# A new opening sequence for a block-sparse attention and mixer kernel, and two normalising steps that both read PSUM

## The chip, the cores and the metric

The kernel runs on one core of a Trainium2 chip. The metric is the device time of one execution in microseconds: 315.58 as the median of 13 runs before the change (314.32 to 317.63).

TensorE (PE in the profile) multiplies matrices into PSUM, VectorE (DVE) and ScalarE (ACT) read PSUM and write SBUF, GpSimd (POOL) works on SBUF alone, and SyncE (SP) issues most of the DMA transfers. Each engine executes its instructions in the order of its own queue.

## The reference

Two stages follow each other. Attention first, for 4 batches, 8 heads, 768 positions and head size 64, with positions in 24 blocks of 32:

```
scores = q k^T / 8
mask   = neighbouring blocks, first and last block (as row or column), 3 sampled blocks per row block
attn   = softmax(where(mask, scores, -1e9))
x      = attn v                      # heads side by side: [4, 768, 512]
```

Then a mixer:

```
u   = x + transpose(transpose(x) U V)       # U 768x32, V 32x768
out = u + relu(u w1) w2                      # w1 512x2048, w2 2048x512
```

## The kernel before

**Attention.** The work goes by pairs of heads: 16 pairs, 4 to a batch. The head size of 64 is filled up to 128 rows: 24 rows beside the data hold one-hot rows on the q side and mask rows on the k side, so that the product of the two gives score plus mask bias. For each head there are six "slots" g, each 128 keys: `scores` (L308) multiplies them with all 768 queries, ScalarE takes the exponential into `est`, and `Pair.av` (L344) multiplies `est` with v into the PSUM tile `pav`, of which there is one buffer. Column 64 of v is all ones, so that the sum of the exponentials comes with the product. After the sixth group, VectorE takes the reciprocal (L360), writes the normalised values `xf` in fp32 from PSUM (L362), and casts them to the fp16 tile `xh` (L366). The next head's first `av` matmul waits until `pav` has been read.

**Mixer.** `mix` (L368) multiplies U with `xh`. `ut` (L377) builds the transposed `u` for one pair, in two halves: three matmuls of `xh` against the identity matrix `id16` (a transpose that adds up in fp32), then V times the result of `mix`, all into one PSUM tile, which VectorE casts to `uT` (L390). The MLP of a batch is a list of steps: 32 of `w1` (four matmuls each, relu by ScalarE and VectorE in turn, L409 and L411) and 24 of `w2`; every fourth of the latter ends in an output sum on VectorE (L428) and a store on SP (L429).

**Order.** TensorE's instructions stand in program order (a manual schedule); on the other engines a scheduler orders them, by the order of the program and its own estimate of when each is ready. One loop walks over 192 slots. In each it traces `scores`, then what `plan` holds for the slot, then at most one entry of `mixer` (`mix` at 4 slots after the pair's end, `ut` at 6 and 7), then as many MLP steps of the batch before as are due. `AVSLOT` gives the slot, counted from the head's first, in which each of the six `av` groups stands: 3, 4, 5, 6, 7, 7. In batch 0 there are no MLP steps.

**Loads.** q, k and v come as fp32 and GpSimd casts them to fp16 (L144, L154). Pairs 0 to 5 are transposed by TensorE (`front_pe`, L296, into `qres` and `kres`, two sets), pairs 6 to 15 by DMA transposes that SP issues (`front`, L286). The load buffers are two deep, and a load waits on SP until its buffer is free. GpSimd issues the loads of the weights.

**Opening.** ScalarE's queue issues the sampled blocks and the small constants (mask, block numbers, and the one-hot rows twice); SP issues the identity and pair 0's q and k, one head at a time. Ten matmuls on zeros (L482 to L484) run first on TensorE. VectorE zeroes the first set of `qres` and `kres`, GpSimd the second; VectorE copies the one-hot rows (L189), then runs the mask chain (L194 three times, L199). `first_front` (L204) casts, transposes and copies q or k of one head of pair 0; `mask_rows` (L221) multiplies the mask into the rows of `kres`; `second_set` (L236) copies mask and one-hot rows to the second set.

Of the kernel before, what the change touches and what calls it, by code (L numbers as in the profile page):

```python
# [16 lines left out]
P = 128  # L17
# [3 lines left out]
def kernel(  # L21
# [44 lines left out]
    oh_np = np.zeros((P, T, D), dtype=np.float16)  # L66
    oh_np[cols % P, cols // P, blk] = 1.0

    small_np = np.zeros((D + NB, 2 * NB + 2 + S), dtype=np.float16)
    small_np[:NB] = np.concatenate(  # L70
        [ms_np.view(np.float16), ii[:, None].astype(np.float32).view(np.float16), ohT_np],
        axis=1,
    )
    small_np[D:, 2 * NB + 2 :] = ohT_np
    eye_np = np.eye(P, dtype=np.float16)

    small_dr = nc.inline_tensor(small_np, name="small_const")
# [25 lines left out]
    def psm(shape, dtype):  # L103
        return psmp.tile(shape, dtype, tag="pm", name="pm")
# [3 lines left out]
    small = consts.tile([P, 2 * NB + 2 + S], FP16)  # L108
    ms = small[0:NB, 0 : 2 * NB].bitcast(FP32)
    iota = small[0:NB, 2 * NB : 2 * NB + 2].bitcast(FP32)  # L110
    ohr = small[:, 2 * NB + 2 :]
    ohT = ohr[0:NB]
    sb = consts.tile([P, NB, 3, 2], I32)
    vts = [consts.tile([P, H, T, DV], FP16, name=f"vt{i}") for i in range(2)]
    qst = [consts.tile([P, 2, T, P], FP16, name=f"qst{i}") for i in range(NST)]
# [46 lines left out]
            [NB, NB * 6]  # L162
        ),
    )
    nc.scalar.dma_start(out=small[0 : D + NB, :], in_=small_dr.ap())
    nc.sync.dma_start(out=id16, in_=eye_dr.ap())
    lds = {}
    for h in range(2):
# [6 lines left out]
            )  # L175

    warm = consts.tile([P, 512], FP16)
    nc.vector.memset(warm, 0.0)
    bias = consts.tile([P, 2, D], FP16)
    nc.vector.memset(bias, 0.0)  # L180
    for i, eng in ((0, nc.vector), (1, nc.gpsimd)):
        for res in (qres, kres):
            eng.memset(res[i], 0.0)
    for vt in vts:
        nc.gpsimd.memset(vt[:, :, :, D : D + 1], 1.0)
    nc.gpsimd.memset(Ut, 0.0)
    nc.gpsimd.memset(Vt, 0.0)
    for h in range(2):
        nc.vector.tensor_copy(out=qres[0][mrows[h], h, :], in_=ohr[mrows[h], :])  # L189

    a01 = consts.tile([P, NB], FP32)
    prev = ms
    for r in range(3):
        nc.vector.scalar_tensor_tensor(  # L194
            out=a01[0:NB], in0=sb[0:NB, :, r, 0], scalar=iota,
            in1=prev, op0=ALU.is_equal, op1=ALU.max,
        )
        prev = a01[0:NB]
    nc.vector.tensor_scalar(  # L199
        out=bias[0:NB, :, 0:NB], in0=a01[0:NB, None].broadcast_to([NB, 2, NB]),  # L200
        scalar1=-MASK_BIAS, scalar2=MASK_BIAS, op0=ALU.mult, op1=ALU.add,
    )

    def first_front(h, n):  # L204
        nm, res = (("qld", qres), ("kld", kres))[n]
        copy = nc.scalar.copy if (h, n) == (0, 1) else nc.vector.tensor_copy
        dst = sts[0, nm][:, :, h]
        if h == 0:
            copy(out=dst, in_=lds[nm][:, h])
        else:  # L210
            nc.gpsimd.tensor_copy(out=dst, in_=lds[nm][:, h])
        pt = psm([P, S], FP16)
        for t in range(T):
            nc.tensor.transpose(  # L214
                out=pt[0 : (h + 1) * D, t * P : (t + 1) * P],
                in_=sts[0, nm][:, t, 0 : h + 1].rearrange("p h d -> p (h d)"),
                identity=id16,
            )
        copy(out=res[0][drows[h], h, :], in_=pt[drows[h], :])  # L219

    def mask_rows():  # L221
        pks = [psvp.tile([P, HS], FP32, tag="pv", name="pv"), psm([P, HS], FP32)]
        for c in range(2):
            nc.tensor.matmul(
                pks[c],
                bias[0:NB].rearrange("k a z -> k (a z)"),
                ohT[:, c * HS : (c + 1) * HS],
                start=True, stop=True,
            )
        for h in range(2):  # L230
            for c in range(2):
                nc.vector.tensor_copy(
                    out=kres[0][mrows[h], h, c * HS : (c + 1) * HS], in_=pks[c][mrows[h]]
                )

    def second_set():  # L236
        for h in range(2):
            nc.gpsimd.tensor_copy(out=qres[1][mrows[h], h, :], in_=ohr[mrows[h], :])
            nc.vector.tensor_copy(out=kres[1][mrows[h], h, :], in_=kres[0][mrows[h], h, :])

    def mask_columns():
        def both(ap):
# [93 lines left out]
    class Pair:  # L336
        def __init__(self, i, bt):
            self.b, self.hp = divmod(i, HP)
            self.bt = bt
            self.ests = {}  # L340
            self.xh = xpool.tile([P, T, P], FP16, tag="xh", name="xh", bufs=3)
            self.ch = slice(self.hp * P, (self.hp + 1) * P)

        def av(self, h, g):  # L344

            head = 2 * self.hp + h
            if g == 0:
                self.pav = psvp.tile([P, T, D + 1], FP32, tag="pv", name="pv")
            pav, est = self.pav, self.ests.pop((h, g))
            for sc in range(T):  # L350
                nc.tensor.matmul(  # L351
                    pav[:, sc, :],
                    est[:, sc * P : (sc + 1) * P],
                    vts[self.b % 2][:, head, g, 0 : D + 1],
                    start=(g == 0 and sc == 0), stop=(g == T - 1),
                    skip_group_check=True,
                )
            if g == T - 1:
                rcp = misc.tile([P, T], FP32, tag="rcp", name="rcp")
                nc.vector.reciprocal(out=rcp, in_=pav[:, :, D])  # L360
                xs = self.bt.xf[:, :, head * D : (head + 1) * D]
                nc.vector.tensor_tensor(  # L362
                    out=xs, in0=pav[:, :, 0:D],
                    in1=rcp[:, :, None].broadcast_to([P, T, D]), op=ALU.mult,
                )
                nc.vector.tensor_copy(out=self.xh[:, :, h * D : (h + 1) * D], in_=xs)  # L366

        def mix(self):  # L368
            pa = psm([P, P], FP32)
# [6 lines left out]

        def ut(self, c):  # L377
            pu = psm([P, HS], FP32)
            for j in range(3):
                nc.tensor.matmul(  # L380
                    pu[:, j * P : (j + 1) * P], self.xh[:, 3 * c + j, :], id16,
                    start=(j == 0), stop=False, skip_group_check=True,
                )
            nc.tensor.matmul(  # L384
                pu,
                self.bt.a16[:, self.ch],
                Vt[:, 3 * c : 3 * c + 3, :].rearrange("r t p -> r (t p)"),
                start=False, stop=True, skip_group_check=True,
            )
            nc.vector.tensor_copy(  # L390
                out=self.bt.uT[self.hp][:, c * HS : (c + 1) * HS], in_=pu
            )


    def mlp_steps(b, bt):
# [54 lines left out]

    LAG = 8
    SLOTS = HP * 2 * T
    AVSLOT = (3, 4, 5, 6, 7, 7)
    queue = []
    plan = {}
    mixer = []
# [22 lines left out]
            since_open += 1  # L479

    with tc.manual_schedule(engines={mybir.EngineType.PE}):
        for _ in range(10):  # L482
            pw = psm([P, 512], FP32)
            nc.tensor.matmul(pw, warm[:, 0:P], warm, start=True, stop=True)  # L484
        first_front(0, 0)
        mask_rows()
        first_front(0, 1)
        at(0, lambda: first_front(1, 0))
        at(1, lambda: first_front(1, 1))
        load_v(0)  # L490
        load_qk(1)
        load_v(1)
# [86 lines left out]
```

The softmax here doesn't subtract the row's maximum and nothing guards it: scores larger than these inputs give would overflow.

## Time and profile before

| what | value |
|---|---|
| median of 13 runs | 315.58 us |
| the profiled execution | 315.29 us, span 313.5 us |
| busy share of the span: TensorE, ScalarE, VectorE, GpSimd | 96%, 57%, 42%, 17% |
| first score on TensorE, first exponential on ScalarE | 12.02 us, 12.88 us |
| bytes moved by DMA | 38.15 MB, 122 GB/s on average |

The page cuts the span into 40 equal slices, one digit each: the busy share in tenths. A group line names the source line, the engine, the operation, the tiles written and read, the shapes and the count; then the busy time in us, the mean duration of one in ns, and the idle time of the engine just before such instructions, with what ended it. A timeline line gives start and duration in us, then the same names; an idle time and its cause stand in brackets. PEld is the loading of weights into TensorE, which lies beside its matmuls. The chain that ended last is followed backwards from the last instruction, at each step to what released it.

### The profile page before, as it was taken

What the parts mean: (1) busy time and instruction counts of PE and PEld (TensorE: products, weight loads), DVE (VectorE), ACT (ScalarE), POOL (GpSimd) and SP (SyncE); (2) the same over time, 40 slices, a digit from 0 to 9 for tenths busy, and PEclk for the clock granted to TensorE, in tenths of its full rate; (3) what the DMA queues carried; (4) which work ended last, traced back from release to release, by engine and by line L of the source; (5) the groups of instructions that cost most, each with busy time, mean ns of one, the idle gap of its engine ahead of it and who ended that gap; (6) DMA issues with size and microseconds to landing.
All of it is one profiled execution on the core that took longest, in us unless ns stands there. A gap on an engine that the chain in (4) does not pass through costs nothing.

```text
span 313.5 us, 6739 instructions
## 1 busy us (share of the span) xinstructions
PE 302.0 (96%) x2782; PEld 185.1 (59%) x2782; DVE 132.3 (42%) x273; ACT 180.0 (57%) x259; POOL 54.5 (17%) x73
## 2 busy tenths in 40 slices
PE   5799999999999999999999999999999999999994
PEld 1467766666665655666665655666665555565442
DVE  5757656544433323444442233445342233443111
ACT  2399999567856555677765555686765550332000
POOL 9692754013320203020201102000000000000000
PEclk9599999999999999999999999999999999999999
DMA  7999999999943747080625125070500101000111
GB/s 217 350 313 239 318 170 134 125 206 258 341 153 81 190 94 211 33 185 18 136 70 102 69 70 132 33 102 2 100 2 33 37 33 69 33 3 0 67 69 67
DMA packets 51238, 38.15 MB, mean 122 GB/s; under 512 B 32887, under 2 KB 47591, under 8 KB 51207
## 3 DMA queue, kind: packets, MB, share of 16 engines
q1 hardware_dynamic: 48384, 33.37, 42.5%
q0 software_dynamic: 2688, 4.19, 8.3%
q8 instruction: 22, 0.36, 0.5%
q10 hardware_dynamic: 135, 0.16, 0.2%
q14 instruction: 9, 0.07, 0.1%
HBM read 27.75 MB, written 6.29 MB: 109 GB/s over the span
## 4 chain that ended last, share of the span: by engine, by line
PE 87%; ACT 7%; DVE 2%; DMA 1%; issue 1%; ACTq 0%; DVEq 0%
PE pm L420 26%; PE pm L401 26%; PE psc L313 17%; PE pv L351 9%; ACT est L319 7%; PE pm L371 2%; PE pm L380 2%; PE pm L384 2%; PE pm L418 2%; DMA small<-small_const 1%; DVE a L194 1%; DVE of L428 1%; PE pm L214 1%; DVE qres L189 0%; DVE xf L362 0%
## 5 line engine op out<-in xcount | busy, mean ns | idle before, releaser
L319 ACT ACTIVATE est<-psc 128x768 f16<-128x768 f32 x192 | 151.3, 810 | 65.0 <-PE psc L313 64.7
L420 PE MATMUL pm<-w2t,tT 128*128 128x512 f16 x384 | 95.1, 379 | 0.0
L401 PE MATMUL pm<-uT,w1t 128*128 128x384 f16 x512 | 94.5, 326 | 0.0
L351 PEld LDWEIGHTS <-est 128*128 128x128 f16 x1152 | 55.6, 97 | 21.3 <-DVE xf L362 1.9
L401 PEld LDWEIGHTS <-w1t 128*128 128x128 f16 x512 | 47.0, 98 | 26.7
L351 PE MATMUL pv<-vt,est 128*128 128x65 f16 x1152 | 60.9, 193 | 0.1
L313 PE MATMUL psc<-aq,ak 128*128 128x384 f16 x240 | 58.5, 326 | 0.0
L411 DVE TENSOR_SCALAR tT<-pm 128x384 f16<-128x384 f32 x64 | 35.7, 557 | 47.6 <-PE pm L401 37.9
L420 PEld LDWEIGHTS <-tT 128*128 128x128 f16 x384 | 35.2, 98 | 33.0
L409 ACT ACTIVATE tT<-pm 128x384 f16<-128x384 f32 x64 | 31.3, 489 | 33.1 <-PE pm L401 17.6
L313 PE MATMUL psc<-qres,kres 128*128 128x384 f16 x144 | 35.8, 333 | 2.7 <-ACT kres L219 0.9
L428 DVE TENSOR_TENSOR of<-xf,pm 128x512 f32<-128x512 f32 x24 | 16.5, 687 | 50.7 <-PE pm L420 50.7
L313 PEld LDWEIGHTS <-ak 128*128 128x128 f16 x240 | 23.4, 98 | 21.9
L390 DVE CAST uT<-pm 128x384 f16<-128x384 f32 x32 | 17.7, 553 | 27.5 <-PE pm L384 27.3
L144 POOL CAST qst<-qld 128x768 f16<-128x768 f32 x10 | 8.3, 828 | 97.0 <-DMA aq<-qst 59.3
L360 DVE RECIPROCAL rcp<-pv 128x6 f32<-128x6 f32 x32 | 6.3, 196 | 32.8 <-PE pv L351 32.0
L313 PEld LDWEIGHTS <-kres 128*128 128x128 f16 x144 | 13.7, 99 | 8.7 <-issue 3.5
L362 DVE TENSOR_TENSOR xf<-pv,rcp 128x384 f32<-128x384 f32 x32 | 17.8, 557 | 1.1
L154 POOL CAST vt<-vld 128x768 f16<-128x768 f32 x16 | 13.5, 843 | 23.5 <-PE pv L351 10.4
L366 DVE CAST xh<-xf 128x384 f16<-128x384 f32 x32 | 15.2, 475 | 0.4
L380 PE MATMUL pm<-id,xh 128*128 128x128 f16 x96 | 10.6, 219 | 0.0
L384 PE MATMUL pm<-Vt,a 128*128 128x384 f16 x32 | 10.4, 326 | 0.0
(63 smaller groups left out, 121.4 us busy)
## 6 DMA issues: line engine op xcount, KB each, us to landing
vld<-in_v_dram SPq DMA_DIRECT2D x16, 384.0 KB, 5.3
out_dram<-of SPq DMA_DIRECT2D x24, 256.0 KB, 2.0
qld<-in_q_dram SPq DMA_DIRECT2D x15, 384.0 KB, 4.7
kld<-in_k_dram SPq DMA_DIRECT2D x15, 384.0 KB, 5.5
w1t<-in_moe_w_ch_dram POOLq DMA_DIRECT2D x4, 512.0 KB, 8.3
w2t<-in_moe_w_ch_dram POOLq DMA_DIRECT2D x4, 512.0 KB, 15.2
qld<-in_q_dram SPq DMA_DIRECT2D x2, 192.0 KB, 3.7
kld<-in_k_dram SPq DMA_DIRECT2D x2, 192.0 KB, 3.7
```

Source lines behind the costliest of these rows:

```text
L313: nc.tensor.matmul(psc[:, c, 0:HS], kT[:, h, g * P : (g + 1) * P], qT[:, h, c * HS : (c + 1) * HS], start=True, stop=True,)
L319: nc.scalar.activation(out=est.rearrange("k (c n) -> k c n", c=2), in_=psc[:, :, 0:HS], func=AF.Exp, scale=0.125,)
L351: nc.tensor.matmul(pav[:, sc, :], est[:, sc * P : (sc + 1) * P], vts[self.b % 2][:, head, g, 0 : D + 1], start=(g == 0 and sc == 0), stop= ...
L362: nc.vector.tensor_tensor(out=xs, in0=pav[:, :, 0:D], in1=rcp[:, :, None].broadcast_to([P, T, D]), op=ALU.mult,)
L380: nc.tensor.matmul(pu[:, j * P : (j + 1) * P], self.xh[:, 3 * c + j, :], id16, start=(j == 0), stop=False, skip_group_check=True,)
L384: nc.tensor.matmul(pu, self.bt.a16[:, self.ch], Vt[:, 3 * c : 3 * c + 3, :].rearrange("r t p -> r (t p)"), start=False, stop=True, skip_gr ...
L390: nc.vector.tensor_copy(out=self.bt.uT[self.hp][:, c * HS : (c + 1) * HS], in_=pu)
L401: nc.tensor.matmul(pt, w1t[:, cc, jj * P : (jj + 1) * P], bt.uT[cc][:, c * HS : (c + 1) * HS], start=(cc == 0), stop=(cc == NCC - 1),)
L409: nc.scalar.activation(out=dst, in_=pt, func=AF.Relu)
L411: nc.vector.tensor_scalar_max(out=dst, in0=pt, scalar1=0.0)
L420: nc.tensor.matmul(hold[sc], bt.tT[jj][:, sc * P : (sc + 1) * P], w2t[:, jj, :], start=False, stop=(jj == NJJ - 1),)
L428: nc.vector.tensor_add(out=of, in0=bt.xf[:, sc, :], in1=hold[sc])
```

## The change

The opening is written anew. The small constants hold the one-hot rows once and are issued by SP ahead of everything else. The order of the opening is written by hand for TensorE, VectorE and ScalarE. VectorE zeroes all four tiles of `qres` and `kres`. The cast of q's first head stands ahead of the mask chain. ScalarE copies the one-hot rows of head 0, and one of the four pieces of the mask rows. Matmuls on zeros stand at three places: 8 first, 1 behind the q transposes, 3 behind the k transposes. The second set's one-hot and mask rows are copied by four DMAs on SP.

In `av`, both normalised results are now made from PSUM, the fp16 one first. For pairs 8 to 14 a tile `xT` is filled from `xh` by a DMA transpose on SP; `ut` then leaves the three identity matmuls out, and VectorE adds `xT` as it reads PSUM. `AVSLOT` is 3, 4, 5, 6, 6, 7.

```diff
-    small_np = np.zeros((D + NB, 2 * NB + 2 + S), dtype=np.float16)
-    small_np[:NB] = np.concatenate(
+    small_np = np.concatenate(
...
-    small_np[D:, 2 * NB + 2 :] = ohT_np
...
-    nc.scalar.dma_start(out=small[0 : D + NB, :], in_=small_dr.ap())
+    nc.sync.dma_start(out=small[0:NB, :], in_=small_dr.ap())
     nc.sync.dma_start(out=id16, in_=eye_dr.ap())
...
-    for i, eng in ((0, nc.vector), (1, nc.gpsimd)):
-        for res in (qres, kres):
-            eng.memset(res[i], 0.0)
...
+    def first_cast(h, n, copy):
+        nm = ("qld", "kld")[n]
+        copy(out=sts[0, nm][:, :, h], in_=lds[nm][:, h])
+
+    def first_turn(h, n):
         pt = psm([P, S], FP16)
         for t in range(T):
             nc.tensor.transpose(
...
+    def first_rows(h, n, pt, copy):
+        copy(out=(qres, kres)[n][0][drows[h], h, :], in_=pt[drows[h], :])
+
+    with tc.manual_schedule(
+        engines={mybir.EngineType.PE, mybir.EngineType.DVE, mybir.EngineType.Activation}
+    ):
+        nc.vector.memset(warm, 0.0)
+        nc.vector.memset(bias, 0.0)
+        for res in (*qres, *kres):
+            nc.vector.memset(res, 0.0)
+        pw = pscp.tile([P, 2, 512], FP32, tag="psc", name="psc")
+
+        def keep_warm(n):
+            for _ in range(n):
+                nc.tensor.matmul(pw[:, 0], warm[:, 0:P], warm, start=True, stop=True)
+
+        keep_warm(8)
+        nc.scalar.copy(out=qres[0][mrows[0], 0, :], in_=ohT)
+        first_cast(0, 0, nc.vector.tensor_copy)
+        ptq = first_turn(0, 0)
+        keep_warm(1)
+        prev = ms
+        for r in range(3):
+            nc.vector.scalar_tensor_tensor(
...
+        nc.vector.tensor_scalar(
...
+        first_rows(0, 0, ptq, nc.vector.tensor_copy)
+        first_cast(0, 1, nc.scalar.copy)
         pks = [psvp.tile([P, HS], FP32, tag="pv", name="pv"), psm([P, HS], FP32)]
         for c in range(2):
             nc.tensor.matmul(
...
+        first_rows(0, 1, first_turn(0, 1), nc.scalar.copy)
+        keep_warm(3)
         for h in range(2):
             for c in range(2):
-                nc.vector.tensor_copy(
+                (nc.scalar.copy if (h, c) == (0, 1) else nc.vector.tensor_copy)(
                     out=kres[0][mrows[h], h, c * HS : (c + 1) * HS], in_=pks[c][mrows[h]]
                 )
+        nc.vector.tensor_copy(out=qres[0][mrows[1], 1, :], in_=ohT)
+
+    def first_front(n):
+        first_cast(1, n, nc.gpsimd.tensor_copy)
+        first_rows(1, n, first_turn(1, n), nc.vector.tensor_copy)
 
     def second_set():
         for h in range(2):
-            nc.gpsimd.tensor_copy(out=qres[1][mrows[h], h, :], in_=ohr[mrows[h], :])
-            nc.vector.tensor_copy(out=kres[1][mrows[h], h, :], in_=kres[0][mrows[h], h, :])
+            nc.sync.dma_start(
+                out=qres[1][mrows[h], h, :], in_=small_dr.ap()[:, 2 * NB + 2 :]
+            )
+            nc.sync.dma_start(out=kres[1][mrows[h], h, :], in_=kres[0][mrows[h], h, :])
...
+            self.xT = None
+            if 2 * HP <= i < NPAIR - 1:
+                self.xT = xpool.tile([P, T, P], FP16, tag="xT", name="xT")
...
-                xs = self.bt.xf[:, :, head * D : (head + 1) * D]
-                nc.vector.tensor_tensor(
-                    out=xs, in0=pav[:, :, 0:D],
-                    in1=rcp[:, :, None].broadcast_to([P, T, D]), op=ALU.mult,
-                )
-                nc.vector.tensor_copy(out=self.xh[:, :, h * D : (h + 1) * D], in_=xs)
+                for dst in (
+                    self.xh[:, :, h * D : (h + 1) * D],
+                    self.bt.xf[:, :, head * D : (head + 1) * D],
+                ):
+                    nc.vector.tensor_tensor(
+                        out=dst, in0=pav[:, :, 0:D],
+                        in1=rcp[:, :, None].broadcast_to([P, T, D]), op=ALU.mult,
+                    )
+                if h == 1 and self.xT is not None:
+                    nc.sync.dma_start_transpose(
+                        self.xT, self.xh.rearrange("p t c -> p (t c)")
+                    )
...
-            for j in range(3):
+            for j in range(3 if self.xT is None else 0):
...
-                start=False, stop=True, skip_group_check=True,
-            )
-            nc.vector.tensor_copy(
-                out=self.bt.uT[self.hp][:, c * HS : (c + 1) * HS], in_=pu
-            )
+                start=(self.xT is not None), stop=True, skip_group_check=True,
+            )
+            dst = self.bt.uT[self.hp][:, c * HS : (c + 1) * HS]
+            if self.xT is None:
+                nc.vector.tensor_copy(out=dst, in_=pu)
+            else:
+                nc.vector.tensor_tensor(
+                    out=dst, in0=pu,
+                    in1=self.xT[:, 3 * c : 3 * c + 3, :].rearrange("c t p -> c (t p)"),
+                    op=ALU.add,
+                )
...
-    AVSLOT = (3, 4, 5, 6, 7, 7)
+    AVSLOT = (3, 4, 5, 6, 6, 7)
...
-        for _ in range(10):
-            pw = psm([P, 512], FP32)
-            nc.tensor.matmul(pw, warm[:, 0:P], warm, start=True, stop=True)
-        first_front(0, 0)
-        mask_rows()
-        first_front(0, 1)
-        at(0, lambda: first_front(1, 0))
-        at(1, lambda: first_front(1, 1))
+        at(0, lambda: first_front(0))
+        at(1, lambda: first_front(1))
```

## The prediction

> **What bounds the kernel now.** I read the page's slices first, then the chain that ended last, then a table by stretches, then timelines of the places that the change touches. Slices and chain:
>
> ```profile
> PE   5799999999999999999999999999999999999994
> ACT  2399999567856555677765555686765550332000
> PEclk9599999999999999999999999999999999999999
> PE 87%; ACT 7%; DVE 2%; DMA 1%; issue 1%; ACTq 0%; DVEq 0%
> ```
>
> A slice is 7.84 us. TensorE is full from the third slice to the end; in slices 3 to 7 ScalarE is full beside it; only the first two slices have room. The stretches agree (columns: time, busy PE, PEld, DVE, ACT, POOL, granted clock, DMA share, GB/s):
>
> ```profile
> 8.00:16.00 8.00, 5.92 (x40) 3.64 (x40) 6.07 (x12) 2.98 (x4) 5.29 (x8) 0.57 1.06 350
> 24.00:55.00 31.00, 29.91 (x421) 21.74 (x418) 20.09 (x45) 29.75 (x42) 15.06 (x19) 1.00 1.09 215
> 55.00:265.00 210.00, 209.85 (x1977) 129.60 (x1975) 82.26 (x176) 129.62 (x187) 19.87 (x24) 1.00 0.48 108
> ```
>
> So there are three regimes. Until the first exponential nothing is full: it is a chain of latencies, partly at a clock of 0.57. From there to 55 us ScalarE sets the pace (one exponential per about 0.72 us), with TensorE taking over at pair boundaries. After 55 us TensorE never stops. A microsecond gained at the start is kept to the end if no load is late; one TensorE microsecond removed after 55 us is one off the end.
>
> The start, ScalarE's and VectorE's timelines (start, duration, operation, wait):
>
> ```profile
> 6.32 1.24 DVE L194 SCALAR_TENSOR_TENSOR a<-sb,small 24x24 f32<-24x24 int32 x1
> 7.48 0.34 DVE L209 CAST stqld<-qld 128x384 f16<-128x384 f32 x1
> 7.75 1.52 DVE L194 SCALAR_TENSOR_TENSOR a<-sb,small,a 24x24 f32<-24x24 int32 x2
> 9.31 0.18 DVE L199 TENSOR_SCALAR bias<-a 24x48 f16<-24x48 f32 x1
> ...
> 11.17 0.79 ACT L219 COPY kres<-pm 64x768 f16<-64x768 f16 x1 [5.32 <-PE pm L214]
> 12.88 0.81 ACT L319 ACTIVATE est<-psc 128x768 f16<-128x768 f32 x1 [0.91 <-PE psc L313]
> 14.16 0.81 ACT L319 ACTIVATE est<-psc 128x768 f16<-128x768 f32 x1 [0.47 <-PE psc L313]
> 15.44 0.81 ACT L319 ACTIVATE est<-psc 128x768 f16<-128x768 f32 x1 [0.47 <-PE psc L313]
> ```
>
> The reader is to see the order: wait for the small constants (VectorE idle 2.32 us), two one-hot copies, mask chain to 9.49, mask matmuls from 9.54, k transposes, k rows on ScalarE, scores at 12.02, exponential at 12.88. The q load had landed at 4.83, k's first head at 5.31. The next two exponentials come 1.28 us apart because TensorE runs at half clock until 15.3.
>
> **What the Trainium skill says.** "TensorE: Matmul & The Clock Gate", Part 1: the clock doubles only after a window of about 3.4 us of activity and halves after an idle one. The trace agrees: full at 5.1 to 8.5 us, half until 15.3, in steps of 3.41. "SBUF — State Buffer", SBUF: two separate sides: GpSimd and a VectorE instruction with two SBUF inputs share a port pair under an exclusive lock. The trace agrees: the same 24x24 instruction of L194 takes 0.24 us alone and 1.24 beside a GpSimd copy. "VectorE: DVE Perf Modes", Why PSUM operands drop a tier: an fp32 PSUM operand leaves one element a cycle, so an fp16 output is not cheaper than an fp32 one; L362 shows 0.557 us.
>
> **The change, part by part.**
>
> *Start.* Small constants become 39 KB instead of 141 and go first on SP, so every load behind them issues one slot later (1.15−0.74 = 0.41 us) but has 0.10 MB less ahead (0.3 us at 340 GB/s): q lands at about 4.95, k at 5.4. VectorE takes all four zeroings (4×0.70, over by about 4.1, before q), then the q cast (0.34): 5.3. The one-hot copies leave VectorE and GpSimd; ScalarE's copy (by "ScalarE: Activation LUTs", What ACT_TABLE_LOAD costs, 0.186 + 768×0.83 ns, an estimate of 0.83 us) lies between the table load's end (2.98) and k's landing: nothing, unless the constants land after 4.6, then its lateness delays the k cast. Mask chain: uncontended 3×0.24 + 0.18 + gaps = 1.0, with GpSimd's casts of head 1 (0.50 and 0.71, landing about 5.9 and 6.4) in its way 2.2; I take 1.3, bias at 6.6 against 9.49. Two mask matmuls 0.6, k transposes 0.52 (full clock) to 0.85, take 0.7: 7.9. ScalarE's k rows 0.79: 8.75; the three warming matmuls lie under them. Scores 0.5 to 0.8: first exponential at about 9.5, against 12.88, **−3.4 us**. ScalarE's extra row copy (a 384-wide cast takes 0.49 in L409) lies under the scores; if the scores wait for it, +0.5. The two slots to the third exponential take 1.45 at full clock, 2.56 now; I take 1.95, **−0.6**. Sum −4.0; ends −2.5 (half clock, locked chain) and −5.3.
>
> Does a load stop it? Data needed earlier by 4.0: pair 1's q cast ends at 10.56 and its transposes start at 16.62 (6.1 us of room); v 8.97 against 15.60; Vt's cast ends at 19.05, first used at 27.0 (8 us). The four new SP copies of `second_set` wait for the mask rows (about 8.6), and SP's queue stands behind them: loads of pair 2 issued at 7.89 now go at about 10.3, costing 2.4 of Vt's 8. GpSimd's queue issues the first weight load behind pair 2's k cast, so it slips as much; the weights landed at 33.5 and are first used at 56.5. All fit, with 1.6 us left at worst (Vt). GpSimd loses 2×1.38 of zeroing and 1.8 of copies, before any use.
>
> *Batch 0, normalising.* The fp16 copy now comes from PSUM (0.557) ahead of the fp32 one (0.557) instead of a cast after it, so the PSUM tile of weighted values comes free 0.59 us later. What waits is the next head's first matmul on TensorE:
>
> ```profile
> 32.83 0.20 DVE L360 RECIPROCAL rcp<-pv 128x6 f32<-128x6 f32 x1 [1.98 <-PE pv L351]
> 33.06 0.56 DVE L362 TENSOR_TENSOR xf<-pv,rcp 128x384 f32<-128x384 f32 x1
> 33.67 0.26 PEld L351 LDWEIGHTS <-est 128*128 128x128 f16 x6 [0.18 <-DVE xf L362]
> ```
>
> Four of the eight heads of batch 0 have no room (0.06 to 0.09 us), four have 0.43. The new slot list moves the fifth group of products one slot ahead, so the sixth ends about 0.17 earlier where ScalarE sets the pace. Net 0.42 for the tight heads, of which the next score's wait (0.17) absorbs a part: 4×0.25 = **+1.0**; ends 0 and +2.4 (4×0.59, none absorbed).
>
> *From 55 us.* Of the 24 heads there, all but two that hand over to another head with work behind have 0.86 us or more between L362's end and the next use, more than 0.59. The two at 129 and 200 us stall already, as VectorE takes a `uT` cast and an output sum between:
>
> ```profile
> 197.95 0.20 DVE L360 RECIPROCAL rcp<-pv 128x6 f32<-128x6 f32 x1 [0.99 <-PE pv L351]
> 198.28 0.56 DVE L390 CAST uT<-pm 128x384 f16<-128x384 f32 x1
> 199.15 0.69 DVE L428 TENSOR_TENSOR of<-xf,pm 128x512 f32<-128x512 f32 x1 [0.31 <-PE pm L420]
> 199.87 0.56 DVE L362 TENSOR_TENSOR xf<-pv,rcp 128x384 f32<-128x384 f32 x1
> ```
>
> 2×0.59 = **+1.2** if that order stays, 0 if it goes. VectorE's extra 0.2 us per head is covered by its idle time (61% after 55 us).
>
> *`ut` of pairs 8 to 14.* Three identity matmuls leave each of 14 calls:
>
> ```profile
> 142.01 0.33 PE L380 MATMUL pm<-id,xh 128*128 128x128 f16 x3
> 142.18 0.33 PE L384 MATMUL pm<-Vt,a 128*128 128x384 f16 x1
> ```
>
> Start to start it is 0.17 us (the 219 ns of one is mostly latency): 14×0.17 = **−2.35**. In their place stand seven transposes on SP. The nearest rows are the transposes of twice the size: 1.4 to 1.8 us to issue, landing 3.8 to 4.1 after. I take 0.9 to issue and 3.5 to land. From `xh` ready to VectorE's `uT` step are 5.7 to 6.4 us now, so they are hidden by 1.3 to 2 us if SP is free. Behind a load or store already waiting on SP (at 156.3, 175.3, 193.3, 246.6) they land about 0.5 us late; VectorE then holds relus, which three PSUM buffers cover. I take **+0.3**, ends 0 and +3. The sum read with `xT` costs VectorE as much as the cast did (0.56).
>
> Sum: −4.0+1.0+1.2−2.35+0.3 = −3.85 on a span of 313.5. The profiled execution took 315.29, so 311.4; the median of the runs is 0.3 above it: **311.7 us**.
>
> **Rivals.**
> (B) The start gains only half: the chain is locked by GpSimd, the clock stays low, or scores wait for ScalarE's second copy. For it: the locked 1.24 above, a pause of TensorE between q transposes and bias; against: warming matmuls in that gap. −2.0 in place of −4.0, the rest unchanged: **313.7**.
> (C) The PSUM hold costs nothing and the start gains all: −5.3−2.35 = −7.65, **307.9**; against it stand the measured 0.06 to 0.09 us of room.
> (D) Slower: the `xT` transposes sit on SP behind stores, VectorE waits in front of relus, and TensorE runs out of PSUM buffers. For it: SP holds stores for output sums (170.7 to 182.3). Three buffers of 0.65 us of products each, less the one in use, cover 1.3 us of lateness beyond the room. Without the xT term my sum is −4.15, so it decides from a TensorE loss of (4.15+0.95)/7 = 0.73 us a pair, a lateness of 2.0 us beyond the room; at 2.5 the loss is 7×1.2 = 8.4: +4.3, **319.9**. Against it: a transpose far behind the store would wait for a sum queued after the step that waits for it, and loads end before 160 us.
> (E) Nothing measurable: stalls eat the gain: **315.6**.
>
> **How the numbers follow.** A no-change measurement tells about 0.3%, 0.95 us. Main case 0.58 (309.8 to 313.0), B 0.18 (313 to 314.6), C 0.11 (under 309.8), E 0.05, D 0.08. The range 308.6 to 314.5 leaves out D, E and C's lower half. Faster 0.87, same 0.05, slower 0.08.
>
> **What would show it.** First exponential at 9 to 10 us and half clock gone by about 12; bias before 7; all eight heads of batch 0 with a wait of TensorE for the second normalising step of 0.2 to 0.6 us; 2742 TensorE matmuls (2782−42+2 for warming); no VectorE wait for `xT`. Wrong, if the first exponential comes after 11, if a load keeps GpSimd late for pair 1, or if VectorE waits for `xT` by more than 2 us a pair.

## The result and the profile after

The changed kernel takes 307.69 us as the median of 11 runs (307.25 to 309.41), against 315.69 for the kernel before (48 runs, 314.06 to 318.33). The ratio is 0.9743, 95% interval 0.9722 to 0.9764. The forecast was 311.7 with a range of 308.6 to 314.5: the sign is right, but the gain of 8.0 us is twice the forecast 3.9, and the time lies below the range. The profiled execution took 307.92 us with a span of 306.0, so the spans differ by 7.55 us.

The page of the changed kernel, slices (7.65 us each) and the chain that ended last:

```profile
PE   8999999999999999999999999999999999999995
ACT  3999998486855655777766455777765540332000
PEclk9999999999999999999999999999999999999999
PE 89%; ACT 6%; DVE 3%; issue 1%; ACTq 0%
```

The first two slices of TensorE, 5 and 7 tenths before, are 8 and 9 now, and the clock has no low slice (its records begin at 6.53 us). The same three stretches as before, from the changed kernel's table (columns: time, busy PE, PEld, DVE, ACT, POOL, granted clock, DMA share, GB/s):

```profile
8.00:16.00 8.00, 7.49 (x95) 5.32 (x96) 5.47 (x11) 7.84 (x13) 5.62 (x8) 1.00 1.03 327
24.00:55.00 31.00, 29.56 (x394) 20.76 (x393) 19.93 (x44) 28.31 (x40) 15.67 (x21) 1.00 1.06 239
55.00:265.00 210.00, 209.78 (x1935) 128.27 (x1934) 83.27 (x175) 128.31 (x185) 20.01 (x25) 1.00 0.47 115
```

From 8 to 16 us ScalarE is busy for 7.84 us where it had 2.98, at a clock of 1.00 instead of 0.57. After 55 us TensorE is full as before, so whatever is gained there must be matmuls that are gone.

Where the 7.55 us come from is read by laying the two traces side by side slot by slot: the start of the same `scores` matmul on TensorE, after minus before.

| stretch | after minus before, cumulative | in this stretch |
|---|---|---|
| slot 0 (first score) | −3.93 | −3.93 |
| slot 4 | −5.40 | −1.47 |
| slot 57 (batch 0 and the first slots of batch 1) | −5.09 | +0.31 |
| slot 114 | −5.09 | 0.00 |
| slot 191, behind pairs 8 to 14 | −7.37 | −2.28 |
| end of the span | −7.55 | −0.18 |

Of the 5.40, the first exponential accounts for 4.25 (12.88 to 8.63 us) and the two behind it for 1.15. The last 0.18 is outside the change's reach as far as the trace shows: TensorE's last matmul is 7.37 earlier, and the last store, behind the last output sum, took 3.02 us in place of 3.20.

The start in the changed kernel, timelines of VectorE, then ScalarE (start, duration, operation, wait):

```profile
4.35 0.30 DVE L184 CAST stqld<-qld 128x384 f16<-128x384 f32 x1
...
4.83 0.52 DVE L219 SCALAR_TENSOR_TENSOR a<-sb,small,a 24x24 f32<-24x24 int32 x2
5.38 0.17 DVE L224 TENSOR_SCALAR bias<-a 24x48 f16<-24x48 f32 x1
```

```profile
2.54 1.28 ACT L213 ACT_TABLE_LOAD   x1 [2.54 <-DMA small<-small_const]
...
8.63 8.79 ACT L336 ACTIVATE est<-psc 128x768 f16<-128x768 f32 x12
```

q is cast at 4.35, the mask chain runs without any lock (0.52 us for two of its instructions), the bias stands at 5.55 instead of 9.49, and from 8.63 ScalarE runs twelve exponentials without a gap. The three between which 1.28 us lay before are now 0.71 and 0.69 apart.

### The profile page after: what moved, and what is told of

Its sections match the earlier page's. It is cut to its first block, busy times and chain, and to the rows that moved or that the text cites. A ratio compares the mean times of both kernels' runs of the same rounds, so it can differ in the third digit from the quotient of the medians.

```text
span 306.0 us, 6678 instructions
## 1 busy us (share of the span) xinstructions
PE 298.4 (98%) x2742; PEld 181.1 (59%) x2742; DVE 129.8 (42%) x271; ACT 181.6 (59%) x261; POOL 49.7 (16%) x69
## 4 chain that ended last, share of the span: by engine, by line
PE 89%; ACT 6%; DVE 3%; issue 1%; ACTq 0%
PE pm L433 27%; PE pm L452 27%; PE psc L330 17%; PE pv L371 11%; ACT est L336 5%; PE pm L397 2%; PE pm L450 2%; PE pm L410 1%; PE psc L210 1%; DVE xf L385 1%; DVE xh L385 1%; PE pm L406 1%; DVE of L460 1%; PE pm L189 0%; DVE rcp L380 0%
## 5 line engine op out<-in xcount | busy, mean ns | idle before, releaser
L330 PE MATMUL psc<-qres,kres 128*128 128x384 f16 x144 | 35.1, 325 | 2.0 <-ACT est L336 1.0
L385 DVE TENSOR_TENSOR xh<-pv,rcp 128x384 f16<-128x384 f32 x32 | 17.8, 555 | 0.9
L330 PEld LDWEIGHTS <-kres 128*128 128x128 f16 x144 | 12.8, 97 | 7.5 <-issue 3.4
L418 DVE CAST uT<-pm 128x384 f16<-128x384 f32 x18 | 10.0, 553 | 16.8 <-PE pm L410 16.8
L420 DVE TENSOR_TENSOR uT<-pm,xT 128x384 f16<-128x384 f32 x14 | 7.8, 558 | 12.2 <-PE pm L410 12.2
L141 POOL CAST kst<-kld 128x768 f16<-128x768 f32 x10 | 8.3, 827 | 13.3 <-DMA kld<-in_k_dram 9.0
```

The lines of the kernel that those rows point to most:

```text
L141: last = nc.gpsimd.tensor_copy(out=dst, in_=ld)
L330: nc.tensor.matmul(psc[:, c, 0:HS], kT[:, h, g * P : (g + 1) * P], qT[:, h, c * HS : (c + 1) * HS], start=True, stop=True,)
L385: nc.vector.tensor_tensor(out=dst, in0=pav[:, :, 0:D], in1=rcp[:, :, None].broadcast_to([P, T, D]), op=ALU.mult,)
L418: nc.vector.tensor_copy(out=dst, in_=pu)
```

## The experiments

Each edit is made on the changed kernel and shown against it. "Slot n" is again the start of that slot's score. The four runs of one version lie up to 3.1 us apart, so small terms are read from slots of the profiles, one for each version.

**The normalising alone undone.**

```diff
-                for dst in (
-                    self.xh[:, :, h * D : (h + 1) * D],
-                    self.bt.xf[:, :, head * D : (head + 1) * D],
-                ):
-                    nc.vector.tensor_tensor(out=dst, in0=pav[:, :, 0:D], ...)
+                xs = self.bt.xf[:, :, head * D : (head + 1) * D]
+                nc.vector.tensor_tensor(out=xs, in0=pav[:, :, 0:D], ...)
+                nc.vector.tensor_copy(out=self.xh[:, :, h * D : (h + 1) * D], in_=xs)
```

> The changed kernel (307.69 us) with the normalising of before: fp32 result from PSUM first, then a cast of it to fp16. Theory 1 (the longer hold of the PSUM tile really costs only what the slot-by-slot comparison shows in batch 0, 0.3 us, because the scores queued behind the waiting products stand 0.2 to 0.4 us early): 0.2 to 0.4 us faster than the changed kernel, 307.3 to 307.5, and TensorE's wait for the normalising falls from 3.4 to about 1.9 us. Theory 2 (the hold costs 1.0 us as predicted, and the new slot list gives 0.7 us back): 1.0 us faster, 306.7.

Measured: 309.05 us, ratio 0.9776 (0.9721 to 0.9831); span 306.2, 0.25 longer than with the new normalising. From slot 6 to slot 57 the old order loses 0.14 against the new. A further 0.44 is lost between slots 57 and 129 and none of it in batch 0: `xh` is now the second of the two results, its transpose starts later, and VectorE waits in front of `uT`. In the changed kernel, then in this run, VectorE at pair 9:

```profile
155.26 0.56 DVE L420 TENSOR_TENSOR uT<-pm,xT 128x384 f16<-128x384 f32 x1 [0.22 <-PE pm L410]
```

```profile
156.12 0.56 DVE L418 TENSOR_TENSOR uT<-pm,xT 128x384 f16<-128x384 f32 x1 [1.18 <-PE psc L330]
```

The wait is put down to TensorE, but V's matmul started at 154.90 in the first and at 154.81 in the second; what is later is `xT`, whose transpose was issued at 151.24 instead of 150.48 and whose last packets moved until 155.57 instead of 153.54. (The moment at which it counts as landed isn't recorded in this run.) So the new order costs nothing that shows here, since 0.14 is less than such profiles differ by (see below), and it pays once where a transposed copy waits for it. The forecast had a loss.

**The slot list alone undone.**

```diff
-    AVSLOT = (3, 4, 5, 6, 6, 7)
+    AVSLOT = (3, 4, 5, 6, 7, 7)
```

> The changed kernel with the old slot list (3, 4, 5, 6, 7, 7). Theory 1 (the slot list moves nothing, since the last group ends at the same place in TensorE's order): within 0.3 us of 307.69. Theory 2 (the slot list pays for the longer hold): 0.7 us slower, 308.4, the loss within the first 57 slots.

Measured: 308.61 us, ratio 0.9752 (0.9708 to 0.9797); span 306.5. From slot 6 to slot 57 it loses 0.79 us, and nothing after. The waits between 8 and 57 us, in the changed kernel and then in this run (engine, line, what it waited for: us, times, longest):

```profile
PEld L371 <- DVE xf L385: 2.4, 5, 0.5
```

```profile
PEld L371 <- DVE xf L385: 3.3, 5, 0.7
PE pv L371 <- DVE xf L385: 1.4, 5, 0.3
```

With the old list the next head's products wait for the PSUM tile, on the matmuls too. The slot list keeps most of the longer hold of the tile off TensorE; it gives something with the short hold too, as the next run shows.

**The opening alone**: old normalising, old slot list, no `xT`.

```diff
-            if 2 * HP <= i < NPAIR - 1:
+            if False:
...
-    AVSLOT = (3, 4, 5, 6, 6, 7)
+    AVSLOT = (3, 4, 5, 6, 7, 7)
```

(and the edit of the first experiment)

> The new opening alone: normalising, slot list and identity matmuls as before. If the parts add up as the slot-by-slot comparison has them (start -5.4 us, batch 0 +0.3, transposes -2.35): 309.7 to 310.1 us, and in batch 0 the slots 6 to 57 take as long as in the kernel before. If the new slot list and the new normalising belong together (old slot list with new normalising lost 0.8 us in these slots, new slot list with old normalising nothing): the same time, but then batch 0 here must be as fast as in the changed kernel or up to 0.3 us faster, not 0.65 us slower as plain adding of the two single runs would have it.

Measured: 310.84 us, ratio 0.984 (0.9807 to 0.9874); span 308.9, which is 4.6 below the kernel before. At slot 6 it is ahead of the kernel before by 5.17, at slot 57 by 4.34, flat after. So an earlier start alone gives back 0.83 in batch 0, with nothing of its normalising changed. The four corners, as what is given back between slots 6 and 57 against the kernel before (+0.31 in the changed kernel, the others from their difference to it; this run directly):

| | old slot list | new slot list |
|---|---|---|
| old normalising | +0.83 | +0.45 |
| new normalising | +1.10 | +0.31 |

One profile stands behind each corner of the table. Seven other profiles with the new normalising, the new slot list and a start within 1.1 us of the changed kernel's gave 0.31 to 0.47, so differences of about 0.2 aren't to be leaned on; the difference of 0.4 to 0.8 between the columns is larger. An eighth, with the constants late and so a start 3.6 us later, gave back 0.01.

**The hold made longer**: the fp16 result is written twice, which keeps the PSUM tile one more instruction of 0.56 us.

```diff
                 for dst in (
+                    self.xh[:, :, h * D : (h + 1) * D],
                     self.xh[:, :, h * D : (h + 1) * D],
```

> The changed kernel with the fp16 result written twice, so that the PSUM tile is held 0.56 us longer again in each of the 32 heads. Theory 1 (the hold was absorbed by early scores, and that room is now used up): every one of the four tight heads of batch 0 pays the whole 0.56 and the others most of it, so 2 to 4 us slower in batch 0, and 1 to 2 us at the heads after slot 57 with under 0.56 us of room; 311 to 313. Theory 2 (VectorE's hold is not on the path at all): within 0.5 us of 307.69.

Measured: 319.0 us, ratio 1.0096 (1.0063 to 1.0129), the kernel's own gain and 3 us more gone; span 317.0, +11.07. From slot 6 to 57 it loses 7.67, to 114 another 2.2, to 191 another 1.6. VectorE, then TensorE's weight loads, at one head of batch 0:

```profile
19.84 0.55 DVE L323 COPY qres<-pm 64x768 f16<-64x768 f16 x1
20.32 0.54 DVE L386 TENSOR_TENSOR xh<-pv,rcp 128x384 f16<-128x384 f32 x1
```

```profile
21.37 0.23 PEld L371 LDWEIGHTS <-est 128*128 128x128 f16 x6 [1.59 <-DVE xf L386]
```

VectorE wrote the first fp16 result at 19.17, then its scheduler put a copy of another pair (L323) ahead of the second and of `xf` (20.78). So the hold, from the start of the reciprocal to the end of `xf`, is 2.4 us at this head and 2.2 to 2.4 at all eight of batch 0, with a copy or a cast in between at each, against 1.25 in the changed kernel and 0.79 before. It grew by about 1.1 us, where one instruction more takes 0.56. The forecast's mechanism (a longer hold stalls TensorE in batch 0) is thus real, but it is an edge: the change's own lengthening of 0.46 us stays on the safe side of it with the new slot list, and one step more falls off.

**The transposed copy left out.**

```diff
-            if 2 * HP <= i < NPAIR - 1:
+            if False:
```

> The changed kernel without the DMA transposes of xh: all 16 pairs use the identity matmuls. Theory 1 (42 matmuls of 0.056 us on a full TensorE): 2.35 us slower, 310.0, in steps of 0.17 us at each of 14 places. Rival (the transposes also delay stores or relus and so give part back): less than 1.5 us slower.

Measured: 309.97 us, ratio 0.9807 (0.975 to 0.9865); span 308.3, +2.31. The loss comes in seven steps of 0.33 to 0.34 us, one at each of pairs 8 to 14; 0.07 comes back at slot 154. In the changed kernel VectorE's step of these pairs is this group (count: least, median and largest duration in ns, first and last start):

```profile
L420 DVE TENSOR_TENSOR uT<-pm,xT x14: 557/558/559, 137.5 to 244.2; 128x384 f16<-128x384 f32 x14
```

The sum costs VectorE what the cast did (557 ns), and the three matmuls with `id16` are gone from TensorE.

This run shows one more thing. Its first exponential came at 7.98, yet at slot 5 it was 0.12 later than the changed kernel. TensorE waited 0.27 us for the cast of v on GpSimd, and for that of pair 1's q:

```profile
11.33 0.51 PE L317 MATMUL pm<-id,stqld 128*128 128x128 f16 x6 [0.36 <-POOL stqld L141]
```

Five other profiles whose first exponential came by 8.2 us lost 0.24 to 0.48 at slot 5 as well. The loads and casts of v and of pair 1 are the next limit of the start: an opening that is earlier still meets them.

**The matmuls on zeros**: without the four behind the q transposes and behind the k transposes, and without the first of these alone.

```diff
-        keep_warm(1)
...
-        keep_warm(3)
```

> The changed kernel without the one warming matmul behind the q transposes and the three behind the k transposes; the eight at the start stay. Theory 1 (they keep the clock up and so give about 1 us of the start's gain): half clock in the first slots, third exponential at 11 us or later instead of 10.0, 0.7 to 1.5 us slower than 307.69. Theory 2 (TensorE is busy enough without them, and the loads of v and of pair 1's q set the fifth slot anyway): first exponential 0.3 to 0.6 us earlier, the fifth score within 0.3 us of 11.7, the time within 0.4 us of 307.69.

```diff
-        keep_warm(1)
```

> Only the single matmul on zeros between the q transposes and the mask matmuls is left out; the eight first and the three later ones stay. First theory (this 0.53 us matmul is in the way of the mask matmuls, which are ready at 5.55 us, and the three later ones hold the clock): mask matmuls at about 5.6 in place of 6.04, first exponential at about 8.2 in place of 8.63, and 0.4 us less at the end: 307.3 us. Rival (it is this one that keeps the clock up over the pause): half clock from 7.8 to 11.2 us as in the kernel without either group, and about 0.5 us more: 308.2 us. A third possibility: the gain is lost to the later casts of v and pair 1 on GpSimd, and slot 6 stands where it stood: 307.7 us.

Measured: without all four 308.19 us, ratio 0.9771 (0.9729 to 0.9814); span 306.5. The first exponential comes 0.63 earlier, at 8.00, with a clock that rose at 4.39; but the clock is half again from 7.81 to 11.22, so that the third exponential comes 0.53 later, and that stays to the end. Without the first alone 309.07 us, ratio 0.9775 (0.9722 to 0.9829); in its profile the clock is half until 10.12, and slot 6 comes 1.09 later. The same opening was profiled once more in a run below (transposed copies for pairs 4 to 15), and there slot 0 comes 0.65 earlier. First scores, of this run and of that one:

```profile
8.39 0.85 PE L329 MATMUL psc<-qres,kres 128*128 128x384 f16 x2
```

```profile
7.45 0.50 PE L329 MATMUL psc<-qres,kres 128*128 128x384 f16 x2
```

One opening, two clocks. "TensorE: Matmul & The Clock Gate", Part 1, says that the window by which the clock is granted runs free, so that the moment of the rise depends on where in it the first matmul falls. The traces agree, and by more than the half microsecond that the page gives. Eight of the profiled executions, the changed kernel's among them, share its opening to the letter:

| clock full from, us | 3.97 | 4.98 | 5.15 | 5.20 | 5.47 | 6.09 | 6.53 | 6.57 |
|---|---|---|---|---|---|---|---|---|
| first exponential, us | 7.99 | 7.98 | 8.05 | 8.07 | 8.19 | 8.41 | 8.63 | 8.65 |

The profile of the changed kernel is the seventh. At slot 6 the eight still lie between 0.38 before it and 0.23 behind it, though no longer in this order: where the first exponential was early, casts of v and of pair 1 were what TensorE waited for next. Without the single matmul on zeros a rise at 4.28 gave 7.98, the same as with it at 4.98; it costs nothing that shows where the clock rises early. Three of the four runs without it took 308.98 to 309.29, where ten of the changed kernel's eleven took 308.51 or less, so it may be worth something where the clock rises late; that isn't shown. The group behind the k transposes has the half clock of 7.81 to 11.22 to show for it, in one profile: without it the clock fell again after a rise at 4.39, with it (and without the single one) it stayed up after a rise at 4.28.

**The small constants as before**: 88 rows with the one-hot rows twice, issued by ScalarE.

```diff
-    nc.sync.dma_start(out=small[0:NB, :], in_=small_dr.ap())
+    nc.scalar.dma_start(out=small[0 : D + NB, :], in_=small_dr.ap())
```

> The changed kernel with the small constants as before: 88 rows, issued by ScalarE behind the sampled blocks. Theory 1 (the place of the constants is what lets the mask chain start at 4.6): they land at about 5, the one-hot copy on ScalarE moves to 5.0 to 5.9 and with it the k cast to 6.4, the mask chain ends at 6.1, the first exponential comes 0.5 to 1.0 us later and 0.2 to 1.0 us of it stays. Theory 2 (the order of the opening alone made the gain): within 0.3 us of 307.69.

Measured: 310.07 us (4 runs, 308.45 to 311.21), ratio 0.9815 (0.9774 to 0.9856); the profiled run is the slowest of the four, with a span of 309.3, +3.30, all of it there by slot 4. ScalarE's table load, and TensorE's first scores:

```profile
5.45 1.28 ACT L215 ACT_TABLE_LOAD   x1 [5.45 <-DMA small<-small_const]
```

```profile
10.20 0.85 PE L332 MATMUL psc<-qres,kres 128*128 128x384 f16 x2
```

The order of the change makes ScalarE's first activation wait for the constants, and in this opening the table load waits with it; in the kernel before it started at 1.70 and lay under the loads. The one-hot copy (6.75) and the k cast (7.60, against 4.71) stand behind it, and the first score comes 2.10 later. The other 1.5 up to slot 4 go by at half clock: two score matmuls take 0.85 us in place of 0.50, and the clock rises at 13.60 only (0.3 of the sum comes back in batch 0). The constants' place at the head of the queue was therefore worth 3.3 us in this execution. What the half clock adds depends on the execution too: the median is 2.4 above the changed kernel's, the fastest of the four runs 0.8, and only the slowest was profiled.

**The mask chain ahead of the first cast.** The three lines with q's cast, its transposes and the matmul on zeros are moved behind the chain and its `tensor_scalar`.

```diff
-        first_cast(0, 0, nc.vector.tensor_copy)
-        ptq = first_turn(0, 0)
-        keep_warm(1)
         prev = ms
...
+        first_cast(0, 0, nc.vector.tensor_copy)
+        ptq = first_turn(0, 0)
+        keep_warm(1)
```

> The changed kernel with the mask chain ahead of the q cast on VectorE, as the order was before. Theory 1 (the gain of the start comes from the constants and from a chain without GpSimd beside it; the order matters little): chain 4.5 to 5.4, q cast 5.7, q transposes to 6.4, first exponential 0.4 to 0.9 us later, of which the loads hide a part: 0 to 0.5 us slower. Theory 2 (the order is the main thing): 1.5 us slower or more.

Measured: 309.44 us, ratio 0.9799 (0.9743 to 0.9854), but no run lies near this median: they took 307.85, 307.98, 310.90 and 310.97. The second was profiled, with a span of 306.2; why two took 3 us more stays open. The first exponential comes at 8.69, 0.06 later, and slot 57 0.22 later; its clock rose at 5.30, where the changed kernel's opening, with rises at 5.20 and 5.47, came at 8.07 and 8.19. At an equal clock the order is thus worth some 0.5 to 0.6 us to the first exponential (8.69 less 8.19 to 8.07), of which a part is lost again to the casts; one profile can't say how much.

**More transposed copies**: for pairs 4 to 14; for pairs 4 to 15 with the single matmul on zeros left out; for pairs 6 to 15.

```diff
-            if 2 * HP <= i < NPAIR - 1:
+            if HP <= i < NPAIR - 1:
```

> The transposed copy also for pairs 4 to 7, where SyncE's queue is fuller: it issues two transposes of 7 to 8 us each up to 67.7 us, and loads of v stand between 75 and 86 us. First theory (a copy that lands anywhere up to the VectorE step that adds it costs nothing): four more pairs give 4 x 0.335 = 1.34 us, so 306.4 us, and the score of slot 114 comes 1.0 to 1.3 us earlier than in the changed kernel. Rival (the queue on SyncE decides, the slower case of the prediction): VectorE waits for the copy at about 71 and 87 us by 1 us or more, its relus come late, TensorE waits for them, and slot 114 comes no earlier or later: 307.5 to 310 us.

```diff
-        keep_warm(1)
...
-            if 2 * HP <= i < NPAIR - 1:
+            if HP <= i:
```

> The transposed copy for pairs 4 to 15, and without the single matmul on zeros. First theory: each of five more pairs gives 0.335 us, pair 15 too, as its copy is needed 4.4 us after the fp16 result: -1.7, and the opening -0.4 to +0.5: 305.6 to 306.5 us. Rival for pair 15: nothing stands behind it, TensorE waits for its transposed u, and this pair alone costs 0.5 to 2 us between slot 191 and the end.

Measured: 325.7 us, ratio 1.031 (1.0247 to 1.0373), and 327.15 us, ratio 1.0338 (1.0264 to 1.0411). Both are slower than the kernel before. Up to slot 66 the first of them is 0.26 ahead of the changed kernel, at slot 69 it is 18.57 behind, and that is the whole loss. SyncE's queue, VectorE and TensorE of that run:

```profile
75.49 8.37 SPq L147 DMA_DIRECT2D vld<-in_v_dram  x4
83.95 1.23 SPq L390 DMA_TRANSPOSE xT<-xh  x1
```

```profile
88.58 0.56 DVE L420 TENSOR_TENSOR uT<-pm,xT 128x384 f16<-128x384 f32 x1 [18.97 <-DMA xT<-xh]
```

```profile
89.19 1.44 PE L433 MATMUL pm<-uT,w1t 128*128 128x384 f16 x4 [16.85 <-DVE uT L420]
```

Pair 4's `xh` was ready at 65.58, but its transpose stood on SyncE behind a transpose of k and twelve loads, and was issued at 83.95. The last four of these loads, of v, took SyncE 8.37 us, as they waited for earlier loads of v and their casts on GpSimd. VectorE waited 18.97 us at `uT`, with every relu behind it, and TensorE 16.85 us for PSUM; then the clock was half until 93.89. One copy in one place costs more than the whole change gains. Pairs 5, 6 and 7 took 0.33 to 0.34 each off the loss (0.25 of pair 5's was given back three slots later), so that it falls by 0.67 from slot 75 to 114. Pairs 4 to 15 show the same place and a loss of 21.0 (slot 69: 20.63 behind).

```diff
-            if 2 * HP <= i < NPAIR - 1:
+            if HP + 2 <= i:
```

> The transposed copy for pairs 6 to 15 in place of 8 to 14: pairs 4 and 5 are left out, since their copies would stand on SyncE behind loads of v that wait till 86 us. First theory (a copy that finds SyncE free costs nothing, and each takes 0.335 us from TensorE): pairs 6, 7 and 15 give 3 x 0.335 = 1.0 us, so 306.7 us against 307.7 for the changed kernel, with VectorE waiting nowhere for a copy. Rival (pair 6 or 7 meets a store on SyncE that waits for an output sum, as at 116.6 us): one wait of VectorE of 2 us or more, and no gain or a loss: 308 to 312 us.

Measured: 306.57 us (5 runs, 306.47 to 306.88), ratio 0.9722 (0.9709 to 0.9735); span 305.1. Against the changed kernel slot 90 is 0.22 earlier (clock and start), slot 111 0.80, and TensorE's last matmul 1.14: pairs 6 and 7 gave 0.58, pair 15 gave 0.34. VectorE waited for one copy, at pair 8, with `uT` 0.2 us late and nothing behind it moved. This is the fastest of the versions run, below both kernels; its interval overlaps that of the changed kernel, but all five of its runs lie below the lowest of the other's eleven (307.25).

## Why the prediction was wrong, point by point

The forecast's sum was −3.85 against a measured −7.55. Three terms failed, all to the same side: the start, right in its mechanism but too small; the longer hold in batch 0, too large; and the two handovers, where the order assumed for VectorE didn't stay. By the sum's own terms:

| step | forecast | measured | error |
|---|---|---|---|
| start, to the third exponential | −4.0 | −5.40 | −1.40 |
| batch 0, longer hold of PSUM | +1.0 | +0.31 | −0.69 |
| the two heads at 129 and 200 us | +1.2 | +0.07 | −1.13 |
| `ut` of pairs 8 to 14 | −2.35 | −2.35 | 0 |
| waits for `xT` | +0.3 | 0 | −0.3 |
| end (last store) | none | −0.18 | −0.18 |

**Start: the mechanism was right, the size too small.** The first exponential was put at 9.5 and came at 8.63. q's cast ended at 4.65 instead of 5.3, as q landed in time for a cast at 4.35, against the 4.95 worked out from the longer queue (−0.65). The chain took 0.9 instead of 1.3, since it was over before GpSimd's first cast at 6.00: the earlier q had moved it out of the lock's reach (−0.4, bias at 5.55 instead of 6.6). The mask matmuls lost about half of that again: ready at 5.55, they started at 6.04 behind the matmul on zeros, which the sum had counted at nothing. From there to the first exponential it took 2.59 instead of 2.9 (−0.3). And the two gaps to the third exponential were 1.40 us in all and not 1.95: the clock was full at 6.53, not at about 12 (−0.55). Of these, some 0.3 us either way is what executions of one opening differ by. I had stretched the half clock of before over the new opening, though the change puts matmuls into just those gaps. The end of −5.3 that I gave for this term was where it came out.

**The longer hold in batch 0: right in kind, too large, and most of the relief comes from the slot list.** The tile is held 0.46 us longer (0.79 to 1.25, from the start of the reciprocal to the end of the last reading) and not 0.59. The sum took four tight heads at 0.25 each and gave the slot list only 0.17 us a head. The 2x2 shows the new normalising at +0.27 with the old slot list and at −0.14 with the new one, neither far above the scatter, and the slot list at 0.38 to 0.79. "The eight heads each with a wait of 0.2 to 0.6" was wrong too: the trace shows 2.4 us in five. What is given back in batch 0 at all is in part the price of starting earlier: the opening alone gives back 0.83, and the start that came 3.6 later 0.01.

**The two handovers: the step "2×0.59 if that order stays" failed.** The order did not stay. VectorE in the changed kernel at the second of them:

```profile
191.69 0.20 DVE L380 RECIPROCAL rcp<-pv 128x6 f32<-128x6 f32 x1 [0.81 <-PE pv L371]
191.85 0.56 DVE L420 TENSOR_TENSOR uT<-pm,xT 128x384 f16<-128x384 f32 x1
192.33 0.55 DVE L385 TENSOR_TENSOR xh<-pv,rcp 128x384 f16<-128x384 f32 x1
192.79 0.68 DVE L460 TENSOR_TENSOR of<-xf,pm 128x512 f32<-128x512 f32 x1
193.51 0.56 DVE L385 TENSOR_TENSOR xf<-pv,rcp 128x384 f32<-128x384 f32 x1
```

Before, VectorE idled 0.31 us there in front of the output sum, which waits for TensorE. Now the added fp16 instruction stands ahead of that sum and fills the wait, so the last reading of the PSUM tile ends no later: 2.4 us after the start of the reciprocal, where it was 2.5 before (2.5 and 2.5 at the other handover). The 0.07 is one step at slot 154, which the run without transposed copies doesn't have. The forecast named the outcome ("0 if it goes") and took the other; with two instructions in a row from the scheduler, the first of which can start while the sum can't, filling was the likelier.

**`ut`: right to the hundredth.** The −2.28 up to slot 191, less the step of +0.07, is the forecast −2.35, and it shows again as seven steps of 0.33 to 0.34 in the run without `xT` and as 0.34 for pair 15.

**`xT`: no wait in pairs 8 to 14**, as the main case had it within its ends. The rival that ends slower (D) did not occur in this change, but its mechanism did, with its order of engines: a transpose held on SyncE, VectorE waiting in front of relus, TensorE short of PSUM. It came at pair 4, behind loads of v and not behind a store, at one pair and for 17 us where D had seven pairs at 1.2. What protects the change is its lower bound of pair 8, or at least of pair 6.

**The rivals.** What happened is near case C (hold free, start in full: 307.9, against 307.69), to which I gave 0.11. That the two agree to 0.2 is in part luck: the hold gave back 0.31, and the start and the last store made up for it. Speaking against it I had "the measured 0.06 to 0.09 us of room": a room measured with the old slot list, though the change moves a group of products by one slot. The changed kernel has no more of it: at five of the eight heads the next product follows the last reading by 0.06 us. But the scores, by which ScalarE goes on, lost only 0.31 us by all these waits. The range left half of C out, and with three terms each leaning to the same side its lower end was too high.

**The signs that were named:** the first exponential came earlier than 9 to 10, half clock was gone by 6.5, bias came before 7, TensorE had 2742 matmuls as counted, ScalarE's one-hot copy took the estimated 0.83 us, and VectorE waited nowhere for `xT`. The room for the loads (6.1 us and more) was worked out for a start 4.0 us earlier, and held for that: at 5.4 to 6.1 earlier, the casts of v and of pair 1's q are what TensorE waits for in part of the runs.

## What to carry to other kernels

An engine's queue is a budget of order, not of time: a DMA that is free where its queue is idle costs 18.8 us where loads that wait for buffers stand ahead of it, so each place of a repeated edit is checked on its own, by what its queue is doing at that moment. When a change both lengthens a hold and moves the work that leads up to it, measure the room against the moved schedule and not the old one; and when an instruction is added on an engine whose order a scheduler makes, look first for a wait that it can fill. For the opening of a kernel, ask of each engine what its first instruction waits for, and what stands behind that.

## What the runs showed that I had not expected

- ScalarE's table load (1.28 us) can wait with the activation behind it. It started with the constants' landing, at 2.54 in the changed kernel and at 5.45 with late constants, where the profiled run lost 3.30 us. In the kernel before it started at 1.70, though the activation behind it waited for k until 5.34; what makes the difference isn't shown.
- The clock's rise in one and the same opening lay between 3.97 and 6.57 us in eight executions, and moved the first exponential by 0.67 us; in two profiles of altered openings it came at 10.12 and 13.60 only. A single profile doesn't tell a change of an opening by half a microsecond.
- One instruction of 0.56 us more on a PSUM tile with a single buffer cost 11 us over 31 handovers, 7.7 of them in batch 0, where the step before it had cost nothing that shows with the same slot list: the slack was used up, and VectorE's scheduler put another copy or cast of 0.55 us in between.
